# Four x loads, interleaved PSUM output of two transforms, and a new task order in a spectral-plus-MLP kernel

## The chip, the cores and the metric

One core of one Trainium2 chip. The metric is device time in microseconds (us) of one execution, as the median of several runs. The profile's span, from the first to the last recorded instruction, is about 2 us shorter than that time. A run more than 1.5% above the fastest of its kernel counts as slow.

## The reference

For x of 2048 rows by 512 columns (bf16), the kernel mixes a spectral filter and a dense block with a gate per row:

```python
g = sigmoid((x * gate_w).sum(-1, keepdims=True))
a = irfft2(rfft2(x) * (w_r + 1j * w_i))            # 2048 x 512, over both axes
h = x @ w1 + b1                                      # 512 -> 1792
b = (h * tanh(softplus(h))) @ w2                     # 1792 -> 512
return g * a + (1 - g) * b
```

## The kernel before

All Fourier transforms are matmuls with constant matrices. The names of the stages are used throughout:

- `tr`: transposes of x on TensorE, for the dense block. `bf`: sums and differences of the halves of x.
- `p` and `d`: the forward transform over rows in a tile and over columns. The result goes to DRAM and back (`s1w`, `s1r`), to change the layout.
- `t`, the filter (`p1`, `p2`, `ad`), `it`: the transform over the tiles, the product with w, and its inverse.
- `id` (the inverse of `d`) and `ip` (the inverse of `p`, joined with the gate).
- `mm1`, `exp`/`ln`/`tanh`, `mul`, `mm2`: the dense block in four chunks of 512 rows.

A task graph is built, and one long string, `ORDER`, fixes the order of all tasks, the engine of those that may run on several, and the PSUM buffer of each (three pairs of banks for most stages). The program gives each engine its tasks strictly in that order, with semaphores between them; in the profile of before, for example, TensorE stood 0.78 us in front of a `d` group at 29.91 us until ScalarE's eviction was done.

The parts that the change touches (cuts marked with `# ...`):

```python
XG = [(0, 1), (1, 4), (4, 8), (8, 12), (12, 16)]         # x in five loads, by tiles of 128 rows
LOADS = [..., "x0 x1 x2 w0 w1 x3 w2 x4", ...]            # loads=1: this entry
ld("front", cst[:], d_front[:], 0.7, writes=["cfront"], queue="act")     # 160 KB of constants
# ...
# d: four matmuls of 128 columns, each to its own contiguous quarter
def f_d(e, t=t + i, i=i, b=b2):
    for c in range(4):
        o = 256 * i + 128 * (c % 2)
        ins = e.matmul(bank(b, c // 2)[:, o:o + 128], zu[:, c, t, :], FD[:, c, :], start=True, stop=True)
# its eviction, PSUM -> SBUF: reads in order, writes every second bf16
evac(f"ed{t}", lambda t=t: rD[:, 512 * t:512 * t + 1024].rearrange("p (r q u) -> p u r q", r=8, u=2),
     lambda b=b2: pair(b).rearrange("p (u r q) -> p u r q", u=2, r=8), 1024, ...)
# ...
# id: two accumulated pairs of 256 columns, contiguous; its eviction writes every second bf16 too
ins = e.matmul(bank(b, e_)[:, 256 * i:256 * i + 256], Hm[:, kri, t, e_, :], FDT[:, kri, e_, :],
               start=(kri == 0), stop=(kri == 1))
evac(f"ey{t}", lambda t=t: rA[:, 512 * t:512 * t + 1024].rearrange("p (g i e) -> p e g i", g=4, e=2),
     lambda b=b: pair(b).rearrange("p (e g i) -> p e g i", e=2, g=4), 1024, ...)
```

An eviction (`evac`) is a `tensor_copy` on VectorE or an `activation(Copy)` on ScalarE, as `ORDER` says.

## Time and profile before

| | before |
|---|---|
| time | 144.06 us (three runs, 143.72 to 144.55) |
| span of the profiled run | 141.8 us |
| first 128x512 matmul | 11.4 us |
| first exp | 18.0 us |
| last matmul ends | about 139.2 us |

The head of the page of before: busy time, share of the span and number of instructions of each engine; further down the engines' shares of the chain of waits.

```profile
PE 133.1 (94%) x917; PEld 74.5 (52%) x917; DVE 123.7 (87%) x161; ACT 116.2 (82%) x81; POOL 42.0 (30%) x39
...
PE 72%; ACT 20%; DMA 3%; DVE 1%; issue 1%; SPq 0%; ACTq 0%
```

TensorE is busy 94% of the span, but that figure alone does not say how full it is, because matmuls overlap in the trace: one of 128x512 lasts 379 ns on average, and the next starts after 216. The chain of waits counts each matmul from one start to the next. Here are pieces of it (start in us, length in us, what): the first run of `mm1`, a `d` pair with its eviction, two more `d` pairs, a run of `mm1`, a `tanh` of the last chunk, and the last 256-column halves of `mm2`.

```profile
11.43 12.19 PE ps L879 x56
28.05 0.46 PE ps L636 x8
28.54 1.33 ACT rD L515
30.57 1.32 DVE rD L512
37.73 0.45 PE ps L636 x8
39.91 0.45 PE ps L636 x8
60.99 7.77 PE ps L879 x36
118.51 3.62 ACT uT L903
135.94 0.87 PE ps L928 x8
```

So a 128x512 matmul costs 7.77/36 = 0.216 us, a 128x256 one 0.87/8 = 0.109, a 128x128 one (L636, the `d` transform) 0.45/8 = 0.056. From 11.4 to 98 us TensorE is almost the whole chain, broken by evictions of `d` of 1.32 us each. From 98 to 123 us ScalarE is the chain; TensorE's two longest gaps there are at the edge correction of the spectrum and at the end of the stretch.

TensorE in that stretch, from the timeline of before (start, length, line, shape, count, and in brackets the idle time before it). L858 is `id`:

```profile
100.64 0.20 PE L802 MATMUL ps<-tmp,rD 128*128 128x1 bf16 x2 [0.63 <-DVE tmp L795]
...
114.06 4.67 PE L858 MATMUL ps<-rE,rF 128*128 128x256 bf16 x40
118.57 1.46 PE L928 MATMUL ps<-w_sb,rD 128*128 128x512 bf16 x6
119.87 2.78 PE L858 MATMUL ps<-rE,rF 128*128 128x256 bf16 x24
...
123.48 0.38 PE L954 MATMUL ps<-rA,rft 128*128 128x512 bf16 x1 [0.56 <-ACT rA L515]
```

Forty `id` matmuls start 4.51 us before the next stage does: 0.113 us each.

The evictions in the groups of before (busy us, mean ns of one | idle before). The ones that write every second bf16 are those to rD (`ed`) and rA (`ey`); those to rC write runs of at least 128 neighbouring elements:

```profile
L512 DVE CAST rC<-ps 128x1024 bf16<-128x1024 f32 x8 | 9.6, 1217 | 0.4 <-PE ps L625 0.3
L512 DVE CAST rA<-ps 128x1024 bf16<-128x1024 f32 x7 | 8.6, 1297 | 0.1
L515 ACT ACTIVATE rC<-ps 128x1024 bf16<-128x1024 f32 x8 | 7.8, 1023 | 1.4 <-PE ps L746 1.4
L515 ACT ACTIVATE rD<-ps 128x1024 bf16<-128x1024 f32 x2 | 2.6, 1317 | 2.4 <-PE ps L636 2.4
```

### The profile page before, as it was taken

Reading aid. Unit: us, or ns where it says so; the run is one execution under the profiler, and the core shown is the slowest. Engines: PE = TensorE matmul, PEld = TensorE weight load, DVE = VectorE, ACT = ScalarE, POOL = GpSimd, SP = SyncE. Lnnn points to the kernel's source line nnn. Section 1 sums busy time; section 2 is a strip of 40 time slices with the busy share of each in tenths; the row PEclk is TensorE's granted clock in tenths of the full one; section 3 lists DMA queues with packets and bytes.
Section 4 is the critical chain, followed back from the end, with each engine's and each line's share of the span. In section 5 each row is a group of like instructions: output and inputs, shape, how many; then the busy total and the mean of one; then the engine's idle time right before and its main releaser. Section 6 shows DMA issues by size and latency. Waiting matters only on the chain.

```text
span 141.8 us, 2331 instructions
## 1 busy us (share of the span) xinstructions
PE 133.1 (94%) x917; PEld 74.5 (52%) x917; DVE 123.7 (87%) x161; ACT 116.2 (82%) x81; POOL 42.0 (30%) x39
## 2 busy tenths in 40 slices
PE   5699999969999999999999999999899999899992
PEld 3485445655574444444567444444355686644471
DVE  0468889979999999999999999999999989998771
ACT  3452083999999999999969999999999999996630
POOL 4004707999980405130510051441300000000200
PEclk9999999999999999999999999999999999999999
DMA  4899999979899980299998663300000000000385
GB/s 122 286 374 388 161 166 161 119 126 303 194 417 351 267 186 2 74 323 370 439 235 158 166 165 74 79 0 0 0 0 5 0 0 0 0 5 0 112 306 178
DMA packets 22831, 22.38 MB, mean 158 GB/s; under 512 B 13668, under 2 KB 19684, under 8 KB 22372
## 3 DMA queue, kind: packets, MB, share of 16 engines
q1 hardware_dynamic: 22496, 22.00, 59.6%
q10 hardware_dynamic: 324, 0.23, 0.6%
q8 instruction: 7, 0.11, 0.3%
q14 instruction: 4, 0.03, 0.1%
HBM read 14.89 MB, written 4.19 MB: 135 GB/s over the span
## 4 chain that ended last, share of the span: by engine, by line
PE 72%; ACT 20%; DMA 3%; DVE 1%; issue 1%; SPq 0%; ACTq 0%
PE ps L879 34%; PE ps L928 26%; ACT uT L900 5%; ACT uT L902 5%; ACT uT L903 5%; DMA rA<-in_A_x_dram 3%; PE ps L746 3%; PE ps L625 2%; PE ps L636 2%; PE ps L954 2%; ACT rD L515 2%; PE ps L598 2%; PE ps L716 1%; DVE rD L512 1%; ACT L903 1%; ACT L902 1%
## 5 line engine op out<-in xcount | busy, mean ns | idle before, releaser
L879 PE MATMUL ps<-rX,w_sb 128*128 128x512 bf16 x224 | 50.8, 379 | 0.6 <-DVE rD L512 0.5
L928 PE MATMUL ps<-w_sb,hs 128*128 128x512 bf16 (+1 forms) x182 | 39.3, 363 | 0.0
L879 PEld LDWEIGHTS ps<-rX,w_sb 128*128 128x128 bf16 x224 | 21.4, 98 | 25.3 <-DVE rD L512 0.7
L928 PEld LDWEIGHTS ps<-w_sb,hs 128*128 128x128 bf16 x182 | 17.6, 98 | 17.6
L886 DVE TENSOR_TENSOR hs<-ps,b1f 128x1024 bf16<-128x1024 f32 x21 | 25.2, 1219 | 1.9 <-PE ps L879 1.7
L900 ACT ACTIVATE uT<-hs 128x2048 bf16<-128x2048 bf16 (+1 forms) x12 | 20.3, 1694 | 6.6 <-DVE hs L886 6.1
L902 ACT ACTIVATE uT<-uT 128x4096 bf16<-128x4096 bf16 (+1 forms) x8 | 25.5, 3190 | 0.2
L903 ACT ACTIVATE uT<-uT 128x4096 bf16<-128x4096 bf16 (+1 forms) x8 | 25.5, 3189 | 0.1
L928 PE MATMUL ps<-w_sb,rD 128*128 128x512 bf16 x56 | 13.2, 379 | 0.2
L912 DVE TENSOR_TENSOR hs<-hs,uT 128x1024 bf16<-128x1024 bf16 (+1 forms) x22 | 12.2, 616 | 0.4 <-ACT uT L903 0.3
L945 DVE TENSOR_SCALAR rX<-ps,omg 128x512 bf16<-128x512 f32 (+1 forms) x11 | 7.6, 701 | 3.6 <-PE ps L928 3.4
L611 DVE TENSOR_TENSOR rB<-rA 128x1024 bf16<-128x1024 bf16 (+2 forms) x8 | 4.1, 554 | 6.9 <-DMA rA<-in_A_x_dram 6.9
L512 DVE CAST rC<-ps 128x1024 bf16<-128x1024 f32 x8 | 9.6, 1217 | 0.4 <-PE ps L625 0.3
L962 ACT ACTIVATE tmp<-ps,gcol 128x512 bf16<-128x512 f32 x11 | 7.1, 685 | 3.1 <-PE ps L954 2.4
L966 POOL TENSOR_TENSOR rX<-rX,tmp 128x512 bf16<-128x512 bf16 x1 | 1.2, 1152 | 27.8 <-ACT tmp L962 27.8
L512 DVE CAST rF<-ps 128x1024 bf16<-128x1024 f32 x8 | 9.1, 1208 | 0.0
L515 ACT ACTIVATE rC<-ps 128x1024 bf16<-128x1024 f32 x8 | 7.8, 1023 | 1.4 <-PE ps L746 1.4
L886 DVE TENSOR_TENSOR rD<-ps,b1f 128x1024 bf16<-128x1024 f32 x7 | 8.4, 1219 | 0.5 <-PE ps L879 0.5
L512 DVE CAST rA<-ps 128x1024 bf16<-128x1024 f32 x7 | 8.6, 1297 | 0.1
L512 DVE CAST rD<-ps 128x1024 bf16<-128x1024 f32 x6 | 7.5, 1305 | 1.0 <-PE ps L636 1.0
L928 PEld LDWEIGHTS ps<-w_sb,rD 128*128 128x128 bf16 x56 | 5.1, 98 | 5.5 <-DVE rD L912 0.5
L515 ACT ACTIVATE rX<-ps 128x512 bf16<-128x512 bf16 x8 | 4.6, 596 | 3.9 <-PE ps L598 3.9
(88 smaller groups left out, 178.5 us busy)
## 6 DMA issues: line engine op xcount, KB each, us to landing
scr<-rD SPq DMA_DIRECT2D x4, 512.0 KB, 7.5
rF<-c_m SPq DMA_DIRECT2D x1, 2048.0 KB, 10.0
rE<-scr SPq DMA_DIRECT2D x4, 512.0 KB, 5.5
rB<-c_g SPq DMA_DIRECT2D x1, 2048.0 KB, 11.1
tmp<-rC SPq DMA_DIRECT2D x16, 128.0 KB, 2.5
out_dram<-rX SPq DMA_DIRECT2D x7, 256.0 KB, 2.5
rA<-in_A_x_dram SPq DMA_DIRECT2D x3, 512.0 KB, 9.4
w_sb<-in_B_w_dram SPq DMA_DIRECT2D x2, 768.0 KB, 9.4
```

The source lines that it names most:

```text
L512: return e.tensor_copy(out=o(), in_=i())
L515: return e.activation(o(), i(), AF.Copy)
L746: ins = e.matmul(bank(b, i)[:, 128 * k:128 * (k + 1)], Mm[:, f, :], In[:, f, :], start=True, stop=True)
L879: ins = e.matmul(bank(b, i), w1_sb[:, dt_, 128 * ft:128 * (ft + 1)], xT[:, c, dt_, :, :], start=(dt_ == 0), stop=(dt_ == 3))
L886: return e.tensor_tensor(out=hs[hb][:, ft:ft + 2, :], in0=pair(b).rearrange("p (f s) -> p f s", f=2), in1=b1f[:, ft:ft + 2].unsqueeze(2).t ...
L900: return e.activation(o, hsf[hb][:, 512 * a:512 * b_], fn_)
L902: return e.activation(o, o, fn_, bias=1.0)
L903: return e.activation(o, o, fn_)
L912: return e.tensor_tensor(out=v, in0=v, in1=uv_[:, a:b_, 128 * tl:128 * (tl + 1)], op=ALU.mult)
L928: ins = e.matmul(bank(b)[:, 0:hi - lo], hs[hb][:, ft, 128 * tl:128 * (tl + 1)], w2_sb[:, ft, lo:hi], start=(ft == 0), stop=(ft == NFT - 1))
L945: return e.tensor_scalar(out=bs[:, t, lo:hi], in0=bank(b)[:, 0:hi - lo], scalar1=omg[:, t:t + 1], scalar2=None, op0=ALU.mult)
L962: G.add(f"fa{t}", "act", act(512) + 0.09, lambda e, t=t, b=b, z=z: e.activation(tb(z)[:, 0:512], bank(b), AF.Copy, scale=gcol[:, t:t + 1]) ...
```

## The change

The intent: let the matmul itself do the interleaving of even and odd columns, so that the evictions become plain contiguous copies (1.02 instead of 1.31 us on ScalarE); bring x in four equal loads and get 128 KB of constants out of the way of the first; and search a new order with the new costs.

```diff
-XG = [(0, 1), (1, 4), (4, 8), (8, 12), (12, 16)]
+XG = [(0, 4), (4, 8), (8, 12), (12, 16)]
-LOADS[1] = "x0 x1 x2 w0 w1 x3 w2 x4"
+LOADS[1] = "x0 x1 w0 w1 x2 w2 x3"
-ld("front", cst[:], d_front[:], ..., queue="act")
+ld("cRF", cst[:, 0, :], d_front[:, 0, :], ..., queue="act")
 ld("braw", ...); ld("graw", ...)
+ld("cFD", cst[:, 1:5, :], d_front[:, 1:5, :], ..., queue="act")
-NWARM = 9      # matmuls on zeros, before x lands (after: 13 of 128x256 in 2.95 us)
+NWARM = 13
 # d
-o = 256 * i + 128 * (c % 2)
-ins = e.matmul(bank(b, c // 2)[:, o:o + 128], zu[:, c, t, :], FD[:, c, :], ...)
+o = 256 * (c % 2) + c // 2
+ins = e.matmul(bank(b, i)[:, o:o + 255:2], zu[:, c, t, :], FD[:, c, :], ...)
-evac(f"ed{t}", ... "p (r q u) -> p u r q" ..., ... "p (u r q) -> p u r q" ...)
+evac(f"ed{t}", lambda t=t: rD[:, 512 * t:512 * t + 1024], lambda b=b2: pair(b), ...)
 # id
-ins = e.matmul(bank(b, e_)[:, 256 * i:256 * i + 256], Hm[...], FDT[...], ...)
+ins = e.matmul(bank(b, i)[:, e_:512:2], Hm[...], FDT[...], ...)
-evac(f"ey{t}", ... "p (g i e) -> p e g i" ..., ... "p (e g i) -> p e g i" ...)
+evac(f"ey{t}", lambda t=t: rA[:, 512 * t:512 * t + 1024], lambda b=b: pair(b), ...)
 # bf for tiles (0,1), (1,4) becomes (0,2), (2,4); ORDER is new from end to end (cut)
```

More of the change, by code (lines that the diff above doesn't have):

```diff
@@ L327 @@
 ORDER = """
-front x0 warm0 wrp1 warm::0 wrp0 x1 ones braw ident x2 graw w1_0 w1_1 x3 w1_2 bf0_0:dve tr0::0 bf0_1:dve x4 evx0:act p0::1 wr0s0 bf1_1:dve tr2::1
-wr0s1 tr3::0 evx2:act bf1_0:dve wr0s2 evx3:act tr1::1 p1 evx1:act bf4_1:dve wr1s0 p2::2 p3 tr7::0 bf4_0:dve wr1s1 tr4::1 evx7:act wi0s0 ep0:dve
-evx4:act tr6::0 p4::0 wi0s1 evx6:act p5 tr5::1 wi0s2 tr_b::0 evx5:act ep4:dve mm1_0_2::1 wi1s0 mm1_0_3 wi1s1 ep2:dve xt8 mm1_0_4::0 ev_b mm1_0_5
-h0_2:dve bf8_0:pool mm1_0_0::2 h0_4:dve mm1_0_1 mm1_0_6::1 h0_0:dve bf8_1:pool mm1_0_7 exp0_0 mm1_0_8::0 h0_6:dve mm1_0_12::2 bf12_0:dve mm1_0_13
@@ L332 @@
-bf12_1:dve mm1_0_9 h0_12:dve wip1 wip0 exp0_4 mm1_0_10::1 h0_8:dve mm1_0_11 wrm000:pool p14::2 h0_10:dve d4::0 d5 p15 ed4:act ep14:dve wrm010:pool
-p12::1 p13 exp0_8 mm1_1_6::0 ep12:dve p10::2 xt9 p11 mm1_1_7 wrm100:pool ep10:dve exp0_12 d14::1 d15 ed14:act h1_6:dve p6::2 xt10 p7 wrm111:pool
-ep6:act d0::1 d1 d10::0 ed0:dve d11 ln0_0 d6::2 d7 wim000:pool xt11 ed10:dve mm1_1_12::1 mm1_1_13 ed6:dve wrm101:pool mm1_1_2::0 w2_0 h1_12:dve s1w1
-p8::2 p9 mm1_1_3 w2_1 ep8:dve wim100:pool mm1_1_4::1 ln0_8 mm1_1_5 h1_2:dve d8::2 wrm110:pool d9 h1_4:dve mm1_1_0::0 tanh0_0 mm1_1_1 ldM ed8:dve rft
@@ L336 @@
-wim110:pool d2::1 d3 h1_0:dve gate0::1 s1w2 ed2:dve d12::2 d13 wim011:pool mm1_1_8::0 ed12:dve mm1_1_9 s1w0 tanh0_8 mm1_1_10::1 mul0_0_0:dve mm1_1_11
-mul0_0_2:dve mul0_0_3:dve mm2_0_0_0::0 mul0_0_1:dve mul0_1_1:dve exp1_0 mul0_1_0:dve mm1_2_0::2 mul0_1_3:dve mm2_0_0_1 h1_10:dve mul0_1_2:pool exp1_4
-h1_8:dve mm1_2_1 mm1_2_10::1 zcl0 wim101:dve exp1_8 mm2_3_0_0::1 wrm011:dve s1w3 wim001:dve ez0 mm2_3_0_1 wim111:dve exp1_12 ez10 omg0 o0_0:dve ln1_0
-mm1_2_4::0 o3_0:dve wim010:pool mm2_1_0_0::0 gcol0 wrn1:dve mm2_2_0_0::1 win1:dve wrm001:dve mm2_2_0_1 ln1_8 wrn0:dve s1r0 s1r1 mm2_1_0_1 s1r2
@@ L340 @@
-o2_0:dve wic1:pool wiz1:pool s1r3 wrc0:pool h2_0:dve mm1_2_5 wrz0:pool edge o1_0:act mm1_2_11 ldG h2_4:dve wrc1:pool wrz1:pool tanh1_0 mm1_2_12::2
-h2_10:dve mm1_2_13 mm1_2_2::0 h2_12:dve mm1_2_3 win0:dve mm1_2_6::1 h2_2:dve mm1_2_7 tanh1_8 mul1_0_3:pool mm1_2_8::2 xt12 h2_6:dve t0_0::0 t0_1
-mm1_2_9 mul1_0_2:dve xt13 et0:act t5_0::1 mul1_1_3:dve t5_1 mm2_6_0_0::1 mul1_0_0:dve mul1_1_2:dve sa0::0 mul1_1_0:dve t7_0::0 mul1_1_1:dve et5:act
-sb0 t7_1 t4_0::1 mul1_0_1:dve et7:act t4_1 sa5::1 mm2_6_0_1 sb5 h2_8:dve et4:act sa7::2 t1_0::0 t1_1 sb7 o6_0:dve t2_0::2 exp2_0 t2_1 xt14 et1:dve
@@ L344 @@
-wic0:pool wiz0:pool t3_0::1 t3_1 mm2_5_0_0::0 xt15 p2_0:dve et3:act p1_0:dve t6_0::0 et2:act t6_1 ad_0:dve mm2_5_0_1 p2_5:dve et6:act sa1::0 p1_5:dve
-sb1 mm2_4_0_0::1 ad_5:dve inv exp2_4 p2_7:dve sa2::1 mm1_3_6::1 p1_7:dve sb2 ad_7:dve exp2_8 mm1_3_10::2 p1_1:dve sa3::2 mm1_3_11 sb3 o5_0:dve
-p2_1:pool mm1_3_4::0 exp2_12 h3_10:dve mm1_3_7 ln2_0 mm1_3_8::2 p1_2:dve ad_1:dve mm1_3_9 p2_3:dve sa4::0 mm1_3_5 p1_3:dve sb4 mm2_7_0_0::0 ad_3:dve
-h3_4:dve p2_2:pool sa6::2 sb6 ln2_8 mm2_7_0_1 h3_8:dve mm1_3_0::0 p1_4:dve ad_2:dve mm1_3_1 o7_0:act p2_4:dve mm1_3_2::2 tanh2_0 ad_4:dve mm1_3_3
@@ L348 @@
-p1_6:dve p2_6:dve mm2_4_0_1 h3_0:dve ad_6:pool gate12::0 h3_2:dve mm1_3_12::0 mm1_3_13 h3_6:dve o4_0:act e1::2 es0::1 mul2_0_2:dve es1 tanh2_8
-mul2_0_3:dve mm2_10_0_0::1 mul2_0_1:dve mul2_0_0:dve xp1::0 xp2 ead::2 exp3_0 mul2_1_1:pool zcl12 e2::1 h3_12:dve mm2_8_0_0::0 e3 mul2_1_2:dve ez12
-it3_0::2 exp3_4 mul2_1_0:dve it3_1 it4_0::0 mul2_1_3:dve it4_1 it2_0::1 eit3:dve it2_1 mm2_8_0_1 exp3_8 eit2:dve it1_0::2 it1_1 mm2_10_0_1 eit4:dve
-o8_0:act it7_0::1 exp3_12 it7_1 eit1:dve it0_0::0 it0_1 mm2_9_0_0::0 o10_0:act eit7:dve ln3_0 it6_0::2 eit0:dve it6_1 it5_0::1 it5_1 mm2_11_0_0::1
@@ L352 @@
-eit6:dve eit5:dve mm2_11_0_1 ezb12 id8::0 ez112 omg12 ln3_8 o11_0:dve id9 id0::2 ey8:dve id1 id12::1 id13 ey0:dve id10::0 tanh3_0 id11 ey12:dve id4::2
-id5 mm2_9_0_1 ey4:dve id14::1 ey10:dve id15 id2::2 ey14:dve id3 id6::0 ey2:act id7 mul3_0_2:dve ezr1::1 o9_0:act ip10::2 mul3_0_0:dve mm2_14_0_0::1
-fa10::0 mul3_0_1:dve tanh3_8 mul3_0_3:dve ey6:dve ip4::2 mm2_12_0_0::0 rfs1 ip2::0 fa4::1 fb10:dve ip8::1 mul3_1_0:dve ip12_0 ip14_0 fa2::2
-mul3_1_3:dve ip3::2 mm2_12_0_1 mul3_1_1:dve fa8::0 mul3_1_2:dve fb4:dve ip0::0 ip5::1 fb8:dve mm2_14_0_1 fa0::1 o12_0:dve fa5::0 fb0:pool ip6::0
@@ L356 @@
-o14_0:dve mm2_13_0_0::0 out14 fb2:dve fa6::1 fb5:dve fa3::2 out5 fb6:dve ip11::1 ip1::0 fin11 ip13_0 ip7::2 fa1::0 mm2_13_0_1 fb3:dve out11 fa7::1
-fb1:dve out3 fb7:dve ip9::1 out1 o13_0:dve mm2_15_0_0::1 fa9::2 out7 fb9:dve ip15_0 mm2_15_0_1 out13 out9 mm2_15_256_0::0 o15_0:dve out15_0 ip15_256
-mm2_15_256_1 o15_256:dve out15_256
+ones cRF x0 ident x1 wrp0 braw wrp1 warm0 w1_0 warm::0 graw w1_1 cFD x2 w1_2 x3 wr0s0 wr0s1 tr2::0 bf2_1:dve tr3::1 evx2:act bf2_0:dve wr0s2 evx3:act
+bf0_1:dve tr0::0 wr1s0 bf0_0:dve p2::1 evx0:act tr1::1 bf4_0:dve wr1s1 p3 evx1:act tr7::0 bf4_1:dve ep2:act p0::2 wi0s0 tr4::1 p1 wi0s1 p4::0 ep0:dve
@@ new lines @@
+evx4:act p5 wi0s2 mm1_0_0::1 evx7:act wi1s0 tr_b::1 ep4:dve tr6::0 wi1s1 mm1_0_1 evx6:act xt8 ev_b tr5::0 mm1_0_2::2 h0_0:dve evx5:act mm1_0_6::0
+bf8_0:dve mm1_0_3 bf8_1:dve mm1_0_7 h0_2:dve mm1_0_4::1 h0_6:dve exp0_0 mm1_0_5 mm1_0_10::2 bf12_0:dve h0_4:dve mm1_0_11 bf12_1:pool mm1_0_8::0
+h0_10:dve exp0_4 mm1_0_9 wip0 wip1 mm1_0_12::1 h0_8:dve wrm000:pool mm1_0_13 exp0_8 mm1_1_4::2 h0_12:dve mm1_1_2::0 wrm001:dve exp0_12 d4::1 d5
+wrm010:dve mm1_1_5 xt9 ed4:dve ln0_0 wrm101:pool mm1_1_3 h1_2:dve mm1_1_0::1 xt10 mm1_1_1 wrm111:pool h1_4:dve mm1_1_6::0 h1_0:dve p12::2 xt11 p13
@@ new lines @@
+wim000:pool mm1_1_7 ln0_8 ep12:dve p10::1 p11 ep10:dve w2_0 p8::2 wim011:pool p9 w2_1 ep8:dve d10::1 tanh0_0 d11 gate0::1 wim111:pool ed10:dve d2::2
+d3 h1_6:dve d8::1 d9 wim101:pool ed8:dve d12::0 d13 ed12:dve s1w2 d0::1 wim110:pool ed2:act d1 ed0:act zcl0 p14::0 p15 p6::2 mul0_0_0:dve p7 ldM
+ep6:act mm1_1_8::1 mul0_0_1:dve s1w0 mm1_1_9 mul0_0_3:dve ep14:act mul0_0_2:dve d6::2 d7 tanh0_8 rft d14::0 ed6:dve d15 wim010:pool mm2_2_0_0::0
+h1_8:dve s1w1 mm1_1_10::2 ed14:act wrm100:dve mm1_1_11 mul0_1_0:dve ez0 mul0_1_3:dve mm1_1_12::1 exp1_0 mul0_1_1:dve mul0_1_2:dve mm1_1_13 h1_10:dve
@@ new lines @@
+mm1_2_4::0 exp1_4 mm1_2_5 h1_12:dve mm1_2_0::2 ez10 exp1_8 omg0 wrm110:pool s1w3 gcol0 wrm011:dve mm1_2_1 wim100:dve mm1_2_2::1 exp1_12 wrn1:dve
+mm1_2_3 ln1_0 mm2_2_0_1 wrn0:dve mm2_0_0_0::1 win1:dve o2_0:dve wrc0:pool wrc1:pool mm2_0_0_1 wrz0:pool wim001:dve win0:dve s1r0 mm2_1_0_0::0 s1r1
+ln1_8 s1r2 o0_0:dve wic0:pool wic1:pool s1r3 h2_2:dve mm2_1_0_1 wiz1:pool wiz0:pool edge ldG h2_4:dve mm1_2_6::1 tanh1_0 mm1_2_7 o1_0:dve mm1_2_10::0
+h2_0:dve wrz1:pool mm1_2_11 h2_6:dve mm1_2_8::2 mm1_2_9 h2_10:dve tanh1_8 mm1_2_12::1 mul1_0_0:dve xt12 mul1_0_2:dve t6_0::0 t6_1 mm1_2_13
@@ new lines @@
+mul1_0_3:dve mul1_0_1:dve xt13 mm2_3_0_0::1 et6:act mul1_1_0:dve mul1_1_1:dve exp2_0 mul1_1_2:dve t3_0::0 t3_1 mul1_1_3:dve sa6::0 mm2_3_0_1 sb6
+h2_8:dve xt14 et3:act mm2_6_0_0::0 o3_0:dve exp2_4 sa3::1 h2_12:dve sb3 t5_0::2 t5_1 xt15 t7_0::0 et5:dve t2_0::1 t2_1 exp2_8 t7_1 mm2_5_0_0::1
+p1_6:dve sa5::2 sb5 p2_6:dve et2:act ad_6:dve t4_0::2 t4_1 mm2_6_0_1 p1_3:dve et4:act sa2::0 p2_3:dve sb2 t1_0::1 et7:act ad_3:dve t1_1 t0_0::2
+p2_5:dve t0_1 sa4::1 et1:act mm2_5_0_1 sb4 p1_5:dve inv et0:act o6_0:dve mm1_3_8::0 p1_2:dve mm1_3_6::1 exp2_12 p2_2:dve mm1_3_0::2 ad_2:dve ln2_0
@@ new lines @@
+p2_4:dve sa0::0 mm1_3_1 sb0 p1_4:dve mm1_3_7 ad_4:dve ad_5:dve mm1_3_9 sa1::1 sb1 o5_0:dve mm2_7_0_0::0 sa7::2 h3_8:dve sb7 ln2_8 p2_0:dve
+mm2_4_0_0::1 p1_0:dve p1_1:dve mm1_3_2::0 ad_0:dve p1_7:dve mm1_3_3 tanh2_0 p2_7:dve mm2_4_0_1 ad_7:dve h3_2:dve p2_1:pool mm2_7_0_1 h3_0:dve
+mm1_3_4::0 mm1_3_5 ad_1:pool h3_6:dve o7_0:act mm1_3_12::2 o4_0:act h3_4:dve mm1_3_13 tanh2_8 mul2_0_1:dve e1::1 mm1_3_10::0 mul2_0_2:dve mm1_3_11
+mul2_0_3:dve mul2_0_0:dve mm2_10_0_0::0 es0::0 es1 mul2_1_1:dve exp3_0 mul2_1_2:dve mul2_1_0:dve mm2_9_0_0::1 mul2_1_3:dve xp1::2 exp3_4 xp2 ead::1
@@ new lines @@
+mm2_9_0_1 h3_10:dve h3_12:dve e2::1 exp3_8 mm2_10_0_1 e3 o9_0:dve it5_0::0 it0_0::2 exp3_12 it4_0::1 o10_0:dve it5_1 it0_1 eit5:dve it4_1
+mm2_11_0_0::1 ln3_0 eit0:dve it6_0::0 it6_1 eit4:dve mm2_8_0_0::0 eit6:dve it7_0::2 it7_1 it2_0::1 it2_1 eit7:dve it3_0::0 ln3_8 it3_1 mm2_8_0_1
+eit2:dve it1_0::2 it1_1 eit3:dve mm2_11_0_1 eit1:act o8_0:dve tanh3_0 id2::1 o11_0:dve id3 id12::0 ey2:dve id0::2 id13 id1 ey12:dve id8::1 id9 ey0:dve
+gate12::0 id10::0 id11 ey8:act zcl12 mul3_0_0:dve id14::2 id15 mul3_0_1:dve ey10:act mm2_12_0_0::1 mul3_0_2:dve mul3_0_3:dve ey14:act id4::1 id6::0
@@ new lines @@
+ez12 tanh3_8 id7 ezb12 ez112 omg12 ezr1::2 ey6:dve id5 mm2_13_0_0::0 rfs1 ey4:act mul3_1_1:dve ip7::0 ip9::2 mul3_1_2:dve ip13_0 fa7::0 mm2_13_0_1
+mul3_1_3:dve mul3_1_0:dve fa9::2 ip2::1 o13_0:dve fb7:pool ip4::0 ip3::2 fa2::1 ip12_0 mm2_12_0_1 fb9:pool fa3::0 ip6::1 o12_0:dve ip8::2 fb3:pool
+fa6::2 mm2_14_0_0::0 out13 fb6:dve fa8::0 fb2:dve out7 ip11::1 fa4::2 ip14_0 fb8:dve out3 ip0::2 fin11 mm2_14_0_1 fa0::1 out9 fb4:dve ip10::0 fb0:dve
+o14_0:dve ip1::1 fa10::0 ip5::2 mm2_15_0_0::1 fa1::2 out14 fb10:dve ip15_0 fa5::1 mm2_15_0_1 out11 fb1:dve out1 mm2_15_256_0::0 o15_0:dve fb5:dve
@@ L359 @@
+out15_0 ip15_256 mm2_15_256_1 out5 o15_256:dve out15_256
 """
-LOADS = ["x0 x1 w0 x2 w1 w2 x3 x4", "x0 x1 x2 w0 w1 x3 w2 x4", "x0 x1 w0 x2 w1 x3 w2 x4", "x0 x1 x2 w0 x3 w1 x4 w2", "x0 x1 x2 x3 w0 w1 x4 w2", "x0 x1 x2 x3 x4 w0 w1 w2"]
+LOADS = ["x0 w0 x1 w1 w2 x2 x3", "x0 x1 w0 w1 x2 w2 x3", "x0 w0 x1 w1 x2 w2 x3", "x0 w0 w1 x1 w2 x2 x3"]
 def _build(nc, A_x, A_w_r, A_w_i, B_x, B_w1, B_b1, B_w2, gate_w, out, merge=12, xtp=8, xtl=12, loads=1, finb=11):
@@ L551, in ld_x @@
             a, b = XG[i]
-            return ld(f"x{i}", x_sb[:, a:b, :], xv[:, a:b, :], (0.45 if a == 0 else 0.36 * (b - a) + 0.15 * (a == 1)), writes=[("x", t) for t in range(a, b)], **kw)
+            return ld(f"x{i}", x_sb[:, a:b, :], xv[:, a:b, :], 1.4 + 0.6 * (a == 0), writes=[("x", t) for t in range(a, b)], **kw)
         def ld_w1(i, **kw):
             a, b = W1P[i]
-            return ld(f"w1_{i}", w1_sb[:, :, 128 * a:128 * b], w1v[:, :, 128 * a:128 * b], 0.53 * (b - a), nd=32,
+            return ld(f"w1_{i}", w1_sb[:, :, 128 * a:128 * b], w1v[:, :, 128 * a:128 * b], 0.43 * (b - a), nd=32,
                       writes=[("w1", f) for f in range(a, b)], **kw)
-        ld("front", cst[:], d_front[:], 0.7, writes=["cfront"], queue="act")
+        ld("cRF", cst[:, 0, :], d_front[:, 0, :], 0.2, writes=["cRF"], queue="act")
         ld("braw", braw[0:14, :], B_b1.rearrange("(ft p) -> ft p", p=128), 0.05, writes=["braw"], queue="act")
         ld("graw", braw[14:18, :], gate_w.rearrange("(dt p) -> dt p", p=128), 0.05, writes=["graw"], queue="act")
+        ld("cFD", cst[:, 1:5, :], d_front[:, 1:5, :], 0.6, writes=["cFD"], queue="act")
         for s in LOADS[loads].split():
@@ L576, in _build @@
         for t in range(xtp, xtl):
-            ld(f"xt{t}", xT[:, t // 4, :, t % 4, :], xv[:, t, :], 0.64, cls="f_xt", transpose=True, nd=128, writes=[("xT", t)])
+            ld(f"xt{t}", xT[:, t // 4, :, t % 4, :], xv[:, t, :], 0.64, cls="f_xe" if t < 8 else "f_xt", transpose=True, nd=128, writes=[("xT", t)])
         for i, (a, b_) in enumerate([(0, 8), (8, 14)]):
@@ L606, in _build @@
         t_bf = []
-        for a, b_ in XG:
+        for a, b_ in ((0, 2), (2, 4), (4, 8), (8, 12), (12, 16)):
             w = b_ - a
@@ L626, in f_p @@
                     return ins
-                t_p.append(G.add(f"p{t + i}", "pe", 4 * 0.058, f_p, "pd", reads=[("xu", 0, t + i), ("xu", 1, t + i), "cfront"], writes=[b]))
+                t_p.append(G.add(f"p{t + i}", "pe", 4 * 0.058, f_p, "pd", reads=[("xu", 0, t + i), ("xu", 1, t + i), "cRF"], writes=[b]))
             evac(f"ep{t}", lambda t=t: zu[:, :, t:t + 2, :], lambda b=b: pair(b).rearrange("p (t c f) -> p c t f", t=2, c=4), 1024,
@@ L634, in f_d @@
                     for c in range(4):
-                        o = 256 * i + 128 * (c % 2)
-                        ins = e.matmul(bank(b, c // 2)[:, o:o + 128], zu[:, c, t, :], FD[:, c, :], start=True, stop=True)
-                    return ins
-                t_d.append(G.add(f"d{t + i}", "pe", 4 * 0.058, f_d, "pd", off=0.4, reads=[("zu", t + i), "cfront"], writes=[b2]))
-            evac(f"ed{t}", lambda t=t: rD[:, 512 * t:512 * t + 1024].rearrange("p (r q u) -> p u r q", r=8, u=2),
-                 lambda b=b2: pair(b).rearrange("p (u r q) -> p u r q", u=2, r=8), 1024, [b2], [("y1", t), ("y1", t + 1)], "pd", 0.6, bias="b_pd")
+                        o = 256 * (c % 2) + c // 2
+                        ins = e.matmul(bank(b, i)[:, o:o + 255:2], zu[:, c, t, :], FD[:, c, :], start=True, stop=True)
+                    return ins
+                t_d.append(G.add(f"d{t + i}", "pe", 4 * 0.058, f_d, "pd", off=0.4, reads=[("zu", t + i), "cFD"], writes=[b2]))
+            evac(f"ed{t}", lambda t=t: rD[:, 512 * t:512 * t + 1024], lambda b=b2: pair(b), 1024, [b2], [("y1", t), ("y1", t + 1)], "pd", 0.6, bias="b_pd")
         t_s1w = []
@@ L857, in f_id @@
                         for kri in range(2):
-                            ins = e.matmul(bank(b, e_)[:, 256 * i:256 * i + 256], Hm[:, kri, t, e_, :], FDT[:, kri, e_, :], start=(kri == 0), stop=(kri == 1))
+                            ins = e.matmul(bank(b, i)[:, e_:512:2], Hm[:, kri, t, e_, :], FDT[:, kri, e_, :], start=(kri == 0), stop=(kri == 1))
                     return ins
                 G.add(f"id{t + i}", "pe", 4 * 0.109, f_id, "id", off=off, reads=[("H", q) for q in range(8)] + ["inv"], writes=[b])
-            evac(f"ey{t}", lambda t=t: rA[:, 512 * t:512 * t + 1024].rearrange("p (g i e) -> p e g i", g=4, e=2),
-                 lambda b=b: pair(b).rearrange("p (e g i) -> p e g i", e=2, g=4), 1024, [b], [("yb", t)], "id", off + 0.1, deps=t_fil, bias="b_u")
+            evac(f"ey{t}", lambda t=t: rA[:, 512 * t:512 * t + 1024], lambda b=b: pair(b), 1024, [b], [("yb", t)], "id", off + 0.1, deps=t_fil, bias="b_u")
         t_m1 = {c: [] for c in range(NCH)}
```

## The prediction

> **What bounds it now.** The chain of waits is 72% TensorE, 20% ScalarE. From its pieces, one 128x512 matmul costs 0.216 us (36 in 7.77), a 128x256 one 0.109, a 128x128 one 0.056; by count TensorE has about 125.5 us of issue work in a span of 141.8. The other 16 us, from chain and timeline: about 8.3 before the first big matmul at 11.4 (x lands at 3.8, 5.5, 8.4), 4.1 in three waits for evictions of the d transform (1.32 each), about 2.4 between 98 and 123, where ScalarE's exp/ln/tanh of the last chunk rule the chain and TensorE has 23.2 us of work in 25.6, and 2.1 after the last matmul. ScalarE is a near co-limit: after its first exp at 18.0 it is busy about 110 of the 118.7 us until its last eviction.
>
> **What changes.**
> - Loads: the same bytes, fewer pieces; 128 KB of constants no longer compete with the first x. Estimate from the landings: first x group at about 5.0, second about 8.2. Only six tiles are transposed before the first big matmul, so it starts about 10.2 instead of 11.4, and the first exp about 16.2 instead of 18.0, if w1's first piece has landed.
> - Evictions: the groups table has the strided d and inverse-d evictions at 1.30 us on VectorE, 1.31 on ScalarE; contiguous ones take 1.21 and 1.02. Over sixteen: 1.2 us on VectorE, under 1 on ScalarE.
> - Placement: ten evictions go from VectorE to ScalarE, seven tasks back. My sum: VectorE 123.7 to about 120 busy, ScalarE 116.2 to about 120; its earlier start pays for the 3.6 added.
> - Order: p and d transforms stand together. Walking the queues by hand with the trace's durations, eleven pairs of 0.45 us pass through three PSUM buffers at evictions of 1.0 to 1.2 us; there TensorE loses about what it won at the start. I have the first half ending within 0.3 us of now (45.5). The later gain is the 2.4 us hole: matmul groups now fill the wait at the edge correction.
> - Interleaved output: 64 d and 64 inverse-d matmuls write every second fp32.[...] No matmul of this trace writes so[...]. If the rate halves, my estimate is [...]10 us more on TensorE: d partly hidden behind evictions, inverse d nearly exposed, about +6 net.
>
> **Critical path.** Interleaving free: about 1 us from the start, 1 to 2 from the last third, at most 1 from the d stage, some lost to crowding: 1.5 to 2.5 off, near 142. At half rate: 147 to 149. I give the first about 65%: the new order was built with unchanged matmul costs.
>
> **Predicted: 142.6 us, 80% range 139.3 to 148.5. Faster by over 2%: 0.28; within 2%: 0.50; slower by over 2%: 0.22.**
>
> **What would show each step.** First 128x512 matmul at 10 to 10.5, first exp near 16; d evictions at 1.2 (VectorE) and 1.02 (ScalarE); spacing of the d matmuls (0.45 per 8 now) and inverse-d ones (0.87 per 8 at that size) unchanged or doubled; waits for evictions still in 30 to 42 us; no ScalarE run of 25 us in the chain's last third.
>
> **What would make it wrong.** Half-rate interleaved writes; the crowded p/d stage costing far more or less than my walk; w1 landing late; the tail, where additions now go to the slower Pool engine (1.15 against 0.42 us).

Where text is cut, it rested on things that no trace of this case shows: a ground for expecting a slowdown, and the two factors of the sum for it. That sum came to 10 us: what 64 matmuls of each kind would add. With the lengths measured in before (0.056 and 0.109 us) they come to 64 x 0.056 + 64 x 0.109 = 10.6 us. As for the constants: in the trace of before the load of 160 KB was issued at 0.82 us and took 2.7 us to land, the first x was under way from 0.80 to 3.78, and the DMA engines were 92% busy from 2.0 to 3.8; what that cost the first x was not measured by itself.

## The result, and the profile after

The changed kernel took 149.55 us (four runs, 149.27 to 149.87) where before took 144.22 (the three runs above and a fourth; 143.72 to 144.55): a ratio of 1.0373, with a 95% interval from 1.0334 to 1.0412. It is slower by 3.7%, outside the stated range. (Ratios are computed as the mean time of one kernel's fast runs over that of the other's of the same rounds, so they are not quite the ratio of the medians quoted.)

The head of the page after, and the engines' shares of its chain:

```profile
PE 140.6 (95%) x921; PEld 79.1 (54%) x921; DVE 119.6 (81%) x162; ACT 119.4 (81%) x84; POOL 32.8 (22%) x35
...
PE 90%; DVE 6%; POOL 1%; issue 1%; ACT 0%; POOLq 0%
```

TensorE became busier by 7.5 us with the same work but for four more of the `NWARM` matmuls, and ScalarE left the chain altogether. VectorE and ScalarE came out as summed beforehand (about 120 each). The evictions did what the change wanted:

```profile
L512 DVE CAST rA<-ps 128x1024 bf16<-128x1024 f32 x4 | 4.8, 1222 | 5.0 <-PE ps L858 5.0
L515 ACT ACTIVATE rA<-ps 128x1024 bf16<-128x1024 f32 x4 | 4.1, 1023 | 5.7 <-PE ps L858 5.7
L515 ACT ACTIVATE rD<-ps 128x1024 bf16<-128x1024 f32 x3 | 3.1, 1018 | 0.4 <-PE ps L637 0.4
```

But VectorE and ScalarE now wait 5.0 and 5.7 us for `id` (L858), where before they hardly waited. Pieces of the chain after, `d` (L637) and `id` (L858):

```profile
8.46 0.67 PE ps L626 x12
9.13 0.86 PE ps L878 x4
...
23.61 0.87 PE ps L637 x8
...
43.18 1.73 PE ps L927 x8
44.91 8.63 PE ps L878 x40
...
114.59 7.01 PE ps L858 x32
121.61 0.38 PE ps L716 x16
121.99 3.48 PE ps L858 x16
125.46 1.73 PE ps L927 x8
127.19 2.59 PE ps L858 x12
129.78 0.22 PE ps L838 x4
130.00 0.86 PE ps L858 x4
130.87 1.73 PE ps L927 x8
...
144.75 0.48 DVE rX L944
```

`id` costs 7.01/32 = 0.219 us per matmul and 8 `d` matmuls cost 0.87 us: twice as much as before, in both. The contiguous matmuls beside them kept their pace (8.63/40 = 0.216). The start, on the other hand, improved more than predicted: the first 128x512 matmul starts at 9.0 us (8.97 in the timeline) instead of 11.4, and the first exp at 15.4 instead of 18.0.

### The profile page after: what moved, and what is told of

It reads as the page before. It is cut to its first block, busy times and chain, and to the rows that moved or that the text cites. A ratio compares the mean times of both kernels' runs of the same rounds, so it can differ in the third digit from the quotient of the medians.

```text
span 147.3 us, 2340 instructions
## 1 busy us (share of the span) xinstructions
PE 140.6 (95%) x921; PEld 79.1 (54%) x921; DVE 119.6 (81%) x162; ACT 119.4 (81%) x84; POOL 32.8 (22%) x35
## 4 chain that ended last, share of the span: by engine, by line
PE 90%; DVE 6%; POOL 1%; issue 1%; ACT 0%; POOLq 0%
PE ps L927 33%; PE ps L878 31%; PE ps L858 9%; PE ps L637 4%; PE ps L819 2%; PE ps L746 2%; DVE hs L885 2%; PE ps L535 2%; PE ps L953 2%; PE ps L626 2%; DVE rC L512 2%; PE ps L599 2%; DVE rD L512 1%; PE ps L716 1%; PE ps L935 1%
## 5 line engine op out<-in xcount | busy, mean ns | idle before, releaser
L944 DVE TENSOR_SCALAR rX<-ps,omg 128x512 bf16<-128x512 f32 (+1 forms) x15 | 10.7, 718 | 4.9 <-PE ps L927 4.7
L858 PE MATMUL ps<-rE,rF 128*128 128x256 bf16 x64 | 14.5, 419 | 0.0
L965 POOL TENSOR_TENSOR rX<-rX,tmp 128x512 bf16<-128x512 bf16 x3 | 3.5, 1152 | 38.2 <-ACT tmp L961 37.9
L858 PEld LDWEIGHTS ps<-rE,rF 128*128 128x128 bf16 x64 | 8.4, 134 | 5.0 <-DVE rF L512 0.4
L515 ACT ACTIVATE rC<-ps 128x1024 bf16<-128x1024 f32 x10 | 9.8, 1022 | 1.1 <-PE ps L746 1.0
L763 POOL TENSOR_TENSOR tmp<-tmp,rA 128x1024 bf16<-128x1024 bf16 x1 | 2.0, 1968 | 31.8 <-DVE rC L766 31.8
L512 DVE CAST rA<-ps 128x1024 bf16<-128x1024 f32 x4 | 4.8, 1222 | 5.0 <-PE ps L858 5.0
L612 DVE TENSOR_TENSOR rB<-rA 128x1024 bf16<-128x1024 bf16 (+1 forms) x9 | 4.7, 568 | 5.2 <-DMA rA<-in_A_x_dram 5.0
L637 PE MATMUL ps<-cst,rC 128*128 128x128 bf16 x64 | 7.8, 311 | 1.0 <-DVE rC L512 0.5
L515 ACT ACTIVATE rA<-ps 128x1024 bf16<-128x1024 f32 x4 | 4.1, 1023 | 5.7 <-PE ps L858 5.7
```

Of the source, the lines that this page charges most:

```text
L512: return e.tensor_copy(out=o(), in_=i())
L515: return e.activation(o(), i(), AF.Copy)
L637: ins = e.matmul(bank(b, i)[:, o:o + 255:2], zu[:, c, t, :], FD[:, c, :], start=True, stop=True)
L858: ins = e.matmul(bank(b, i)[:, e_:512:2], Hm[:, kri, t, e_, :], FDT[:, kri, e_, :], start=(kri == 0), stop=(kri == 1))
L944: return e.tensor_scalar(out=bs[:, t, lo:hi], in0=bank(b)[:, 0:hi - lo], scalar1=omg[:, t:t + 1], scalar2=None, op0=ALU.mult)
```

## The experiments

**Theory A:** a matmul that writes every second fp32 of PSUM runs at half rate, in this kernel on the critical path; everything else in the change is neutral or good. **Theory B (rival):** the doubled `id` and `d` partly hide behind evictions and ScalarE; what costs is the new order, with its crowded `p`/`d` stage and other placement of evictions. If A holds, a second question follows: is it the step as such, or that no two neighbouring fp32 are written together? The two predict different things for pairs of elements with gaps between the pairs, which e5 separates.

| run | kernel | us, median | ratio to before of its rounds (95%) |
|---|---|---|---|
| e1_inverse_d_back | after, `id` contiguous | 142.86 | 0.984 (0.979 to 0.990) |
| e2_d_back | after, `d` contiguous | 148.89 | 1.027 (1.021 to 1.034) |
| e3_both_back | after, both contiguous | 142.02 | 0.981 (0.974 to 0.988) |
| e4_old_order_interleaved | before, both interleaved | 152.30 | 1.052 (1.043 to 1.060) |
| e5_pairs | after, pairs of fp32 interleaved | 141.77 | 0.985 (0.982 to 0.989) |
| e6_contiguous_matmul_permuted_read | after, matmul contiguous, eviction reads out of order | 141.47 | 0.983 (0.980 to 0.987) |
| e7_d_step_four | e1 with step four in `d` | 143.05 | 0.994 (0.990 to 0.999) |
| e8_old_order_permuted_read | before with e6's eviction | 144.32 | 1.003 (0.995 to 1.011) |
| e9_after_again | after | 149.43 | 1.038 (1.033 to 1.043) |
| e10_best_again | e6 | 141.48 | 0.983 (0.977 to 0.988) |
| e11_best_old_loads | e6 with the old loads | 144.06, four of six runs slow | 0.983 (0.974 to 0.993), from its two fast runs |

All gave correct results. e1 to e4 shared a chip, e5 to e8 another, e9 to e11 a third. On the first, before took 145.09 (median of seven, 144.22 to 146.96), so times of different groups are best compared by ratio, and those of one group directly. Some runs of before in these rounds were slow (one of seven, three of seven, two of eleven); they are in its medians, but not in the ratios.

### e1 to e3: undoing the interleaved writes

Edit of e1 (e2 does the same for `d`, with the two lines of `d` of the kernel before; e3 does both):

```diff
-ins = e.matmul(bank(b, i)[:, e_:512:2], Hm[...], FDT[...], ...)
-evac(f"ey{t}", lambda t=t: rA[:, 512 * t:512 * t + 1024], lambda b=b: pair(b), ...)
+ins = e.matmul(bank(b, e_)[:, 256 * i:256 * i + 256], Hm[...], FDT[...], ...)
+evac(f"ey{t}", ... "p (g i e) -> p e g i" ..., ... "p (e g i) -> p e g i" ...)
```

> The kernel after, with only the inverse-d matmuls writing contiguous halves again and their evictions strided again, as before; order, loads and d stay. Theory A (the interleaved write halves the matmul rate, and the inverse-d stage is exposed): the 64 matmuls go from 0.219 to 0.109 us each, 7.0 us of TensorE work goes, and the time falls by 5 to 7 us, to 142.5 to 144.5; the eight evictions go back to 1.30 us. Theory B (the new order is what costs; the doubled matmuls hide behind ScalarE): under 2.5 us falls, 147 or more.

> The kernel after, with only the d matmuls contiguous and their evictions strided again. Theory A: 8 d matmuls take 0.45 us again instead of 0.87, 3.4 us of TensorE work goes, of which I expect half on the path, because the d pairs wait for evictions anyway: 147.3 to 148.7. Theory B (the crowded p/d stage is bound by evictions): the slower evictions make it no better or worse, 149 to 150.5.

> The new order and the new loads alone: both transforms contiguous, both evictions strided. Theory A: the order is good, 140.5 to 142.5, faster than before by 1 to 2.5%. Theory B: 145 or more, slower than before.

Measured: 142.86, 148.89 and 142.02 us. Within this group, `id` alone costs e2 minus e3 = 6.9 us, and `d` alone costs e1 minus e3 = 0.8 us. e1 and e3 landed where theory A put them. e2 lies just over A's range and just under B's, so `d` gives back less than half of its work; three of its four runs also ran at a lowered clock (below). Theory B is out as the cause of the loss: the new order with contiguous matmuls is faster than before, by 1.9%. For `d` alone its point about hiding holds in part (see the section on the clock).

The group of `id` in e1 (first fence) and in after (second) shows the mean length of one matmul, 272 and 419 ns. It is longer than the spacing in the chain (0.109 us, 12 in 1.31, in e1, and 0.219 in after), and grows by 147 ns where the spacing grows by 110, so it less than doubles where the spacing doubles:

```profile
L858 PE MATMUL ps<-rE,rF 128*128 128x256 bf16 x64 | 7.8, 272 | 0.0
```

```profile
L858 PE MATMUL ps<-rE,rF 128*128 128x256 bf16 x64 | 14.5, 419 | 0.0
```

The `id` evictions in e1 were back at 1.31 us (VectorE) and 1.32 (ScalarE), and nothing was lost by that: ScalarE and VectorE no longer stood waiting (0.0 and 0.3 us before them instead of 5.7 and 5.0).

### e4: the interleaved writes in the old order

The edit puts the two `+` pairs of the change for `d` and `id` into the kernel before, and nothing else.

> The kernel before, with only the interleaved writes and contiguous evictions of both transforms put in; old order, old loads. Theory A: 7.0 us for the inverse d less the 2.4 us hole that the old order has there, and some 1 to 3 us for d: 149 to 152. Theory B: within 1.5 us of before, 144 to 146.

Measured: 152.30 us, 7.2 us over before, a ratio of 1.052. Theory A again, slightly over the range. The expectation that `id` would grow into the 2.4 us hole was mostly wrong: the greater part of that hole lies before `id` starts. In the timelines, from the first `id` matmul to the first of `ip` it takes 133.56 - 118.23 = 15.33 us in e4 and 123.48 - 114.06 = 9.42 in before, 5.9 more, so only 0.9 of the 6.8 us of added `id` work (0.216 us each in e4's chain, 0.109 in before) found room. From the first 128x512 matmul to the first of `mm2`, the part with `d`, it takes 2.7 us more. (The profiled run of e4 was its slowest, 153.88 us, and its first 128x512 matmul started 1.2 us later than in before, at 12.66 instead of 11.43 in the chains; its wait for the third x load ended at 8.98, that of before at 8.38.)

### e5: pairs of fp32

Each matmul writes two neighbouring fp32 and skips two, so that each 8 bytes hold two results of one matmul. The eviction reads PSUM in the order j, s, e and writes SBUF contiguously; `d` is done the same way.

```diff
-ins = e.matmul(bank(b, i)[:, e_:512:2], Hm[...], FDT[...], ...)
-evac(f"ey{t}", ..., lambda b=b: pair(b), ...)
+ins = e.matmul(bank(b, i).rearrange("p (j e s) -> p e j s", e=2, s=2)[:, e_], Hm[...], FDT[...], ...)
+evac(f"ey{t}", ... "p (j s e) -> p j s e" ..., lambda b=b: pair(b).rearrange("p (j e s) -> p j s e", e=2, s=2), ...)
```

> The kernel after, with both interleaved outputs at a grain of two fp32 (8 bytes) instead of one: each matmul writes two neighbouring columns and skips two; the evictions read PSUM in the permuted order and still write SBUF contiguously. [...]inverse d 0.109 us per matmul, d 0.45 us per 8, and the time about that of both transforms put back, 141 to 143. If any step other than one halves the rate (the access pattern itself), spacing stays 0.219 and the time stays near 149. The evictions: 1.22 and 1.02 us if reading out of order is free, about 1.3 if not.

The first branch says of the times that pairs run at the contiguous rate.

The pieces of e5's chain:

```profile
41.19 0.46 PE ps L637 x8
...
113.95 3.65 PE ps L859 x32
...
121.52 1.31 PE ps L859 x12
```

The rate of contiguous writes: 0.114 us per `id` matmul in the first piece and 0.109 in the last, and 0.46 us for 8 of `d` (0.109 and 0.45 in before). The time is 141.77 us. So it is not the step as such: two fp32 together, 8 bytes, sufficed here. All pairs here begin on an 8-byte boundary; pairs that do not were not run.

### e6: the eviction reads out of order

```diff
 # id (d alike, with 128-column pieces)
-ins = e.matmul(bank(b, i)[:, e_:512:2], Hm[...], FDT[...], ...)
-evac(f"ey{t}", ..., lambda b=b: pair(b), ...)
+ins = e.matmul(bank(b, i)[:, 256 * e_:256 * e_ + 256], Hm[...], FDT[...], ...)
+evac(f"ey{t}", ... "p (x n e) -> p x n e" ..., lambda b=b: pair(b).rearrange("p (x e n) -> p x n e", x=2, e=2), ...)
```

> The new order with contiguous matmul outputs, where the eviction does the interleaving by reading PSUM out of order and writing SBUF contiguously (instead of reading in order and writing with a step). Matmuls at 0.109 and 0.056. If it was the stepped SBUF write that cost 1.30 us, the evictions take 1.22 (VectorE) and 1.02 (ScalarE), and the time is a little under that of both put back: 141.0 to 142.0, the fastest so far. If reading PSUM out of order costs as much, 1.3 or more and 142 or more.

Measured: 141.47 us, and the evictions in its groups:

```profile
L512 DVE CAST rA<-ps 128x1024 bf16<-128x1024 f32 x4 | 4.8, 1223 | 1.0 <-PE ps L859 0.8
L515 ACT ACTIVATE rA<-ps 128x1024 bf16<-128x1024 f32 x4 | 3.9, 1020 | 0.0
```

So what made the old evictions slow was the stepped write into SBUF: with every second bf16 written they took 1.30 us on VectorE and 1.31 on ScalarE in before. Reading PSUM with jumps of 1 KB between neighbouring elements took no longer here than reading it in order, on either engine: 1.22 and 1.02 us, as for the evictions to rC in the same run (1.22 and 1.02). Done by the read of the eviction, the interleaving cost nothing in these times.

Its chain, from the end of the `p`/`d` stage and around `id`, to be set beside that of after:

```profile
33.62 3.62 ACT uT L904
37.23 1.83 ACT rD L515 x2
...
41.91 1.73 PE ps L929 x8
43.63 3.88 PE ps L880 x18
...
113.32 3.60 PE ps L859 x32
...
122.37 0.44 PE ps L859 x4
122.81 1.73 PE ps L929 x8
...
136.70 0.48 DVE rX L946
```

The order is the same in both kernels, so the same piece of work can be compared. The first `mm2` piece (8 matmuls) ends at 43.63 here and at 44.91 in after: 1.28 us are lost up to the end of the `d` stage. From the first `id` to the last it takes 122.81 - 113.32 = 9.49 us here and 130.87 - 114.59 = 16.28 in after: 6.79 us. Together 8.07, and the last scaling of an output starts 144.75 - 136.70 = 8.05 later. That is the whole difference.

### e7: step four

`d` writes every fourth fp32 (the four matmuls fill a bank between them); `id` is contiguous, as in e1.

```diff
-o = 256 * (c % 2) + c // 2
-ins = e.matmul(bank(b, i)[:, o:o + 255:2], zu[:, c, t, :], FD[:, c, :], ...)
+ins = e.matmul(bank(b, i)[:, 2 * (c // 2) + c % 2:512:4], zu[:, c, t, :], FD[:, c, :], ...)
```

> As e1 (inverse d contiguous), but the d matmuls write every fourth fp32 instead of every second. [...]step four costs what step two does: 0.87 us per 8 d matmuls, time as e1, 142.5 to 143.5. If the cost grows with the step, 1.7 us per 8, and 2 us or more slower than e1. The d evictions read with a step of 8 bytes and write contiguously: 1.22 and 1.02 us if that is free.

In the chain of e7, 8 `d` matmuls take what they take at step two:

```profile
23.53 0.87 PE ps L636 x8
```

The time is 143.05 us, in the expected band. (The ratio of 0.994 against e1's 0.984 comes from two chips; I rest nothing on it.) So `d` matmuls that write single fp32 took twice the time of contiguous ones (0.45 us per 8 in before), at step two and at step four alike.

### e8: what the intent was worth

> The kernel before, with only the evictions of both transforms changed: same matmuls (the pieces of a bank moved), reading PSUM out of order and writing contiguously. If the evictions become 1.22 and 1.02 us, this is what the change wanted without its cost; about 1.3 us less on VectorE and 0.9 on ScalarE, of which the three waits of d evictions (1.3 each in the chain) and the inverse d give at most 1 us: 143.0 to 144.3 beside before in the same rounds, a ratio of 0.990 to 1.000.

The edit is e6's, applied to the kernel before. The evictions became 1.22 us (VectorE) and 1.02 (ScalarE), as in this group of e8:

```profile
L515 ACT ACTIVATE rD<-ps 128x1024 bf16<-128x1024 f32 x2 | 2.0, 1024 | 2.4 <-PE ps L636 2.4
```

But the time stayed: 144.32 beside 144.09 (the fast runs of before: 143.49 to 144.09), a ratio of 1.003 (0.995 to 1.011), just outside the expected band on the side of no gain. A gain of 0.5% cannot be excluded, but none is seen. In the new order it is the same: e3 (stepped evictions) and e6 (contiguous ones) stand at 0.981 and 0.983 of before. Sixteen cheaper evictions were worth nothing that these times can show, even free of charge. The traces of the new order do have two of them in the chain, the two `d` evictions of ScalarE at 37.3 us, with 2.39 us in e3 and 1.83 in e6; a gain of that size, 0.56 us or 0.4%, is within the intervals.

### e9 to e11: the distance on one chip, and the loads

> The changed kernel itself, on the same chip as the next two, for a clean distance. 149 to 150.5; ratio to before 1.03 to 1.04.

> The same kernel as e6 (new order and loads, contiguous matmul outputs, evictions that read out of order), with more rounds: 141.2 to 142.2, ratio to before 0.979 to 0.987, and 7.5 to 8.5 us under e9.

> As e10, but x in five loads (one tile, three, then fours) and the constants in one piece, as before; the order of work stays. If the larger loads and the split constants earn the start: the first group of four tiles lands at 5.5 instead of 5.0 to 5.4, the first 128x512 matmul about 0.3 us later, the time 0.2 to 0.6 us over e10. If the start was earned by the order alone (four tiles first, the first big matmul after six transposes): within 0.2 us of e10.

e9: 149.43 us, e10: 141.48, as expected; the interleaved writes cost 7.95 us. e10 beats before by 1.75% (0.977 to 0.988 of it) and after by 5.3%.

e11 is e6 with x in five loads and the constants in one, as before. It is inconclusive. Its six runs were 141.16, 142.00 and then 143.58 to 146.26, four of them slow. The two fast ones lie where e10 lies, so the fast runs show no gain of the loads. The one trace of e11 is of a slow run (144.53): in it TensorE waited for the second four tiles of x until 9.36 us, and the first 128x512 matmul started at 11.14, against 9.13 in e10. So whether the gain at the start comes from the loads or from the order stays open. Whether the large loads make the kernel steadier (e10's six runs lie within 1.1 us, and those of before in the same rounds within 3.5) was not tested further and stays open.

### A side observation: the clock in the `p`/`d` stage

In e2, TensorE's granted clock fell in the middle of the kernel. Stretches of 4 us of e2 (busy us of each engine with the number of instructions, then the clock, the DMA share and GB/s):

```profile
30.00:34.00 4.00, 3.30 (x81) 2.83 (x78) 4.00 (x5) 3.97 (x3) 3.83 (x3) 0.98 1.02 325
34.00:38.00 4.00, 3.43 (x28) 2.56 (x28) 3.97 (x6) 4.00 (x2) 3.85 (x3) 0.50 0.47 140
38.00:42.00 4.00, 3.58 (x25) 2.40 (x24) 2.87 (x4) 3.93 (x5) 1.57 (x2) 0.66 0.95 223
```

The longest wait of TensorE just ahead of it was 0.59 us. Three of four runs of e2 and of e3, and one or two of e5, e6, e10 and e11, had a mean clock of 0.974 to 0.988; e1, e7, after and e9, with their slower `d` matmuls, and before, e4 and e8, in the old order, had 0.998 or more in every run. What sets the fall off stays open: in the profiled runs of e3 and e6 TensorE was busy for the same 3.30 us from 30 to 34, then for only 2.27 and 2.44 us from 34 to 38, and the clock stayed at 1.00. Where it happened it cost little: e2's run at full clock took 148.51, the others 148.75 to 149.82.

So the half-rate `d` writes cost 3.4 us of TensorE work but only 0.8 us (e1 against e3, medians) to 1.3 us (e6 against after, both at full clock) of time. The chains show where the rest hides. In e6, as in e3 and e10, ScalarE is the chain from about 21.5 to 39 us: exp, ln and tanh of the first chunk, then two `d` evictions (the last pieces are in the fence under e6), and TensorE has room meanwhile. In after, TensorE and VectorE are the chain in this stretch.

## Why the prediction was wrong

- **The step that failed: "Interleaving free", held for about 65% likely because "the new order was built with unchanged matmul costs".** The writes run at half rate: 0.219 instead of 0.109 us per `id` matmul, 0.87 instead of 0.45 per 8 of `d` (profile after), and e1 to e4 show that this alone turns a gain of 1.9% into a loss of 3.7%. No trace that the prediction had showed such a write; what it rested on was a guess about what the author of the change knew. The costs that a scheduler works with are assumptions, not measurements.
- **The size of that branch was low as well.** "About +6 net", 147 to 149, was 7.95 us (e9 against e10). `id` was put down as nearly exposed and is fully so, 6.8 to 6.9 us; `d` was put down as partly hidden and is (0.8 to 1.3 of 3.4).
- **"Interleaving free: near 142" was right.** e3 and e6, the change without interleaved writes, took 142.02 and 141.47.
- **The start was better than predicted.** First big matmul at 9.0 us (predicted 10.2), first exp at 15.4 (16.2); in e9, the same kernel, 9.6 and 16.1. The first x group landed at 5.05 in the profile after, as predicted (5.0); the second, estimated at 8.2, was already being transposed at 7.63.
- **"There TensorE loses about what it won at the start" was right as a sum, in part by luck.** In e6, counting the sixteen matmuls of `mm1` left over and the `mm2` piece done early, the first half ends at 43.63 - 1.73 + 3.46 = 45.36 us, before at 45.45. But more was won and lost than predicted (about 2 us each way instead of 1.2), and the path was not the walk through three PSUM buffers: it was ScalarE's exp, ln and tanh, with two evictions queued behind them.
- **The 2.4 us hole was right in size.** In e6 the edge correction is filled with matmul groups, and the last matmul ends at 136.67 instead of 139.23, 2.56 earlier, 2.47 of it after the first half. Only about 0.8 us of the hole lay at the edge correction (in the timeline of before, eight matmuls from 98.11 on take 1.73 us, and the next one starts at 100.64); 0.7 lay at its end, and the rest in waits of about 0.3 us or less.
- **Evictions: the durations were right.** 1.22 and 1.02 us came as said; e8 shows no gain from them.
- **The tail on Pool** is not in the chain: after and e6, with three additions there (one in before), both end on TensorE and VectorE. Its cost was not measured by itself.

## What to carry to other kernels

When an operand must be permuted on its way through PSUM, let the read of the eviction do it, as in e6: the matmul writes contiguously (or two fp32 together, as in e5; 0.109 us here instead of 0.219) and the copy writes SBUF contiguously (1.22 and 1.02 us instead of 1.30 and 1.31). When a change bundles a new cost with a new order, measure its one unproven assumption by itself before counting on it, since a single matmul group of 64 was enough to undo a good order. And before making an eviction cheaper, ask who waits for it: sixteen cheaper ones bought nothing that could be measured here.
